# Reordering the low halves of h and splitting a weight's conversion between two engines, in a mixer kernel on one core

## The chip, the core and the metric

One core of a Trainium2 chip runs the whole program. The metric is the device time of one execution in microseconds (us). The kernel before has a median of 408.17 us over three runs (408.06 to 408.4).

The engines are named as the profile names them: PE (TensorE, matrix multiply), PEld (its weight loads), DVE (VectorE), ACT (ScalarE), POOL (GpSimd) and SP (SyncE, which here issues every DMA transfer; its queue is called SPq). Each engine works through its own list of instructions in order and waits at an instruction until the semaphores that it names have been raised.

## The reference, cut to what matters

```python
xn = _layernorm(x, axis=-1)                        # x: 1 x 2048 x 448
return x + A(xn, w_r, w_i) + B(xn, w1, w2, w3, w4)

# A: rfft2 of xn, times (w_r + 1j * w_i), irfft2
# B:
h  = gelu(_layernorm(x) @ w1)                      # 448 -> 448
# the four quarters of h are shifted by +1, -1, +2, -2 tokens -> hs
x1 = x + hs @ w2                                   # 448 -> 448
h2 = gelu(_layernorm(x1) @ w3) @ w4                # 448 -> 1792 -> 448
return x1 + h2
```

The change lies in the early part of B: the first normalisation, the product with w1, the shift, and the product with w2.

## The kernel before, in words

**Numbers in two halves.** Matrix products take fp16 operands. Every fp32 operand is split into a high half, its fp16 rounding, and a low half, the fp16 rounding of what is left. ACT usually writes the high half, and DVE or POOL subtracts it to get the low half.

**Blocks and groups.** The 2048 tokens stand in 16 blocks of 128 (token 16a + b is row a of one block), so that a shift by one or two tokens moves data from block to block, and only at the two ends from row to row. `GRP` puts the blocks in four groups of four: 14, 15, 0, 1, then 2 to 5, 6 to 9, and 10 to 13. The change speaks of the second group, blocks 2 to 5, and of the end of the first.

**One group's way.** `norm1(g)` takes statistics on DVE and ends in a scale and an offset for each block (`nma`, L328); the four blocks are then normalised by DVE and POOL (L336) and ACT (L333). Its second part, `refine`, computes the exact scale `gsc` on POOL (L343 to L352). `T1(g)` transposes the group on PE (L389), ACT takes the high half out of PSUM (L393) and DVE the low half (L394), into `xT`. Group 3 goes another way, `turn(3)`: ACT and DVE write halves of each block (L860 to L862), and a DMA transpose moves them to `xT` (L863).

**`w1_unit(g, i)`** multiplies block i of group g with w1 (11 matmuls, L420), then ACT computes gelu in place (L459) and the high half of h (L460). DVE computes the low half in two instructions (L462), k = 0 and k = 1. Both halves land shifted: `slots_of` spreads the four quarters of block c over the memory slots c-2, c-1 (k = 0) and c+1, c+2 (k = 1) of `x2mem`. A slot b is complete when its four neighbours have delivered. `DONE` names which slots are complete after which block, and for these the unit issues a DMA transpose on SP into `hT` (L470). So transpose 0 needs low halves from units (0,0) and (0,1), the first half of (0,3) and the first half of (1,0). It needs nothing from (0,2) itself.

**`w2_tile(b)`** multiplies the transposed slot b with w2: 11 matmuls (L478), the first six with the high and low halves of w2's first three pieces, then the low half of the fourth, then four with the pieces w2p[3] to w2p[6]. These four are copies of high halves, set together by two DMA moves inside `w2p` (L924, L925). DVE adds the product to x (L479), with a scale `cs` that POOL computes (L360 to L365). Tiles alternate between two PSUM banks, so tile 2 must wait until DVE has emptied the bank of tile 0.

**w2's halves.** POOL scales each piece (L276), ACT writes its high half (L277), POOL subtracts (L278). The four pieces are done in a row before the second group's units, and both moves are queued right behind them on SP.

**What sets the order.** Instructions are put on each engine's list by a scheduler that follows priorities and the order of the code; `behind(key)` keeps an instruction from being issued before another one has been. SP's list is in one order too, and a DMA transpose that waits holds back all transfers behind it. Behind the four transposes of the second group stand the loads of the last part of w3 (L223, two of 448 KB) and of w4 (L238, 1344 KB), and behind these the transposes of `turn(3)` and those of the next four slots.

Of the kernel before, what the change touches and what calls it, by code (L numbers as in the profile page):

```python
# [15 lines left out]
AF = mybir.ActivationFunctionType  # L16
ALU = mybir.AluOpType
# [108 lines left out]
def body(tc, nc, x, wf, w1, w2, w3, w4, c_g, c_n, c_small, out):  # L126
    V, A, P, T, SY = nc.vector, nc.scalar, nc.gpsimd, nc.tensor, nc.sync
# [28 lines left out]
    def bank(tag, name):  # L156
        return ps.tile([128, 512], F32, tag=tag, bufs=2, name=name)
# [19 lines left out]
    def stage(name, n, side, dtype=F32):  # L177
        t = pw.tile([128, 1808], F32, tag=f"stage{side}", bufs=1, name=name)
        return (t if dtype is F32 else t.bitcast(dtype))[:, :n]
# [25 lines left out]
    w2s = stage("w2s", F, 1).rearrange("p (t n) -> p t n", t=4)  # L205
# [49 lines left out]
    def powers(m, n, key, tag="acc", spare=0):  # L255

        t = pc.tile([128, 2], F32, name=f"pt{key}")
        after["r" + key] = (V.tensor_reduce(out=t[:, 0:1], in_=m[:, :n], axis=AX.X, op=ALU.add).ins,)
        pm = bank(tag, f"pm{key}") if isinstance(tag, str) else tag
        i = T.matmul(pm[:, 0:1], ones, t[:, 0:1], start=True, stop=True)  # L260
        after["p" + key] = (i.ins,)
        V.tensor_scalar(out=t[:, 1:2], in0=pm[:, 0:1], scalar1=2.0 ** -58, scalar2=None, op0=ALU.max)
        e = pc.tile([128, 3], I32, name=f"pe{key}")
        V.tensor_scalar(out=e[:, 0:1], in0=t.bitcast(I32)[:, 1:2], scalar1=1, scalar2=0x7F800000,
                        op0=ALU.logical_shift_right, op1=ALU.bitwise_and)
        V.tensor_scalar(out=e[:, 1:2], in0=e[:, 0:1], scalar1=-1, scalar2=185 - spare << 23, op0=ALU.mult, op1=ALU.add)
        i = V.tensor_scalar(out=e[:, 2:3], in0=e[:, 0:1], scalar1=1, scalar2=69 + spare << 23, op0=ALU.mult, op1=ALU.add)
        after["e" + key] = (i.ins,)
        return e.bitcast(F32)[:, 1:2], e.bitcast(F32)[:, 2:3]
# [4 lines left out]
    def split_w(hi, lo, src, s, low=None):  # L274
        if low is P:
            after["ps"] = (P.tensor_scalar(out=src, in0=src, scalar1=s, scalar2=0.0, op0=ALU.mult, op1=ALU.add).ins,)  # L276
            i = A.activation(out=hi, in_=src, func=AF.Copy)  # L277
            j = P.tensor_tensor(out=lo, in0=src, in1=hi, op=ALU.subtract)  # L278
            return i.ins, j.ins
        i = A.activation(out=hi, in_=src, func=AF.Copy, scale=s)  # L280
        j = V.scalar_tensor_tensor(out=lo, in0=src, scalar=s, in1=hi, op0=ALU.mult, op1=ALU.subtract)
        return i.ins, j.ins
# [89 lines left out]
    after = {}  # L372

    @contextlib.contextmanager
    def behind(*key):
        key = key if len(key) > 1 else key[0]
        with contextlib.ExitStack() as st:
            for i in after[key]:
                st.enter_context(tc.issue_after(i))
            yield  # L380
# [27 lines left out]
    w2p = pr.tile([128, 11, D], F16, name="w2p")  # L408
# [5 lines left out]
    def w1_in(g, units, ts, passes=range(3)):  # L414
        for p in passes:
            for t in ts:
                for i, pm in units:
                    wi, xi = ((0, 0), (0, 4), (4, 0))[p]
                    if t < 3 or p != 1:
                        m = T.matmul(pm[:, :D], xTs[g][:, xi + t, 128 * i:128 * i + 128], w1p[:, wi + t],  # L420
                                     start=t == 0 and p == 0, stop=t == 3 and p == 2)
        after["u"] = (m.ins,)

    def slot(b):
        return x2mem[:, 896 * b + 3584:896 * b + 4480].rearrange("p (i n) -> p i n", i=2)

    def slots_of(c, i):

        t = slot(c - 2)[:, i]
        return bass.AP(t.tensor, t.offset, [list(t.ap[0]), [3 * 896 + 224, 2], [896 + 112, 2], [1, 112]])  # L430
# [12 lines left out]
    def wrap_on():  # L443
        move(pairs[1], pairs[0], -1)

    def wrap_back():
        move(pairs[0], pairs[2], 1)
        for b, k in ((-2, slice(224, 448)), (-1, slice(336, 448))):
            P.tensor_copy(out=slot(b)[:, :, k], in_=slot(b - 2)[:, :, k])

    def w1_unit(g, i, pm=None):
        if pm is None:
            pm = bank(("tr" if g == 1 else "mm", "acc")[i // 2], f"pw1_{g}{i}")
            w1_in(g, [(i, pm)], range(4))
        c = CS[GRP[g][i]]
        pm = pm[:, :D]
        pv_ = pm.rearrange("p (i j n) -> p i j n", i=2, j=2)
        h = [slots_of((GRP[g][i] + 2) % NB - 2, k) for k in range(2)]
        A.activation(out=pm, in_=pm, func=AF.Gelu_apprx_tanh, scale=gsc[:, c:c + 1])  # L459
        u = A.activation(out=h[0], in_=pv_, func=AF.Copy, scale=h1)  # L460
        for k in range(2):
            v = V.scalar_tensor_tensor(out=h[1][:, k], in0=pv_[:, k], scalar=h1, in1=h[0][:, k],  # L462
                                       op0=ALU.mult, op1=ALU.subtract)
        after[g, i] = u.ins, v.ins
        for b in DONE.get(GRP[g][i], ()):
            if b == 14:
                wrap_back()
            if b // 4 not in hT:
                hT[b // 4] = pr.tile([128, 7, 512], F16, tag="h", bufs=2, name=f"h{b // 4}")
            d = SY.dma_start_transpose(out=hT[b // 4][:, :, 128 * (b % 4):128 * (b % 4) + 128],  # L470
                                       in_=slot(b if b < 14 else b - 16).rearrange("p i n -> p (i n)"))
            after["h", g, i] = (d.ins,)

    def w2_tile(b):
        pm = bank("sp", f"pw2_{b}")
        h = hT[b // 4][:, :, 128 * (b % 4):128 * (b % 4) + 128]
        for n, (k, w) in enumerate([(k, w) for k in range(3) for w in (k, k + 7)] + [(3, 10)] + [(k, k) for k in (3, 4, 5, 6)]):
            T.matmul(pm[:, :D], h[:, k], w2p[:, w], start=n == 0, stop=n == 10)  # L478
        V.scalar_tensor_tensor(out=xb(b), in0=xb(b), scalar=cs[:, CS[b]:CS[b] + 1], in1=pm[:, :D],  # L479
                               op0=ALU.mult, op1=ALU.add)  # L480
# [367 lines left out]
    def T1(g, ts=range(4)):  # L848
        if g not in xTs:
            xTs[g] = p1.tile([128, 7, 512], F16, tag="xT", bufs=2, name=f"xT{g}")  # L850
        transpose_split([xb(b) for b in GRP[g]], xTs[g], f"a{g}", ts,
                        tags=("mm", "mm", "tr", "tr") if g == 2 else ("tr", "tr", "acc", "acc"))
# [26 lines left out]
    first = [bank("mm" if k < 2 else "sp", f"pw1_0{k}") for k in range(4)]  # L879
# [9 lines left out]
    n = 2  # L889
# [11 lines left out]
    with behind("n", 1), behind("u"):  # L901
        s2, r2 = powers(m2, 1, "2", first[0][:, 448:512])
# [9 lines left out]
    for k in range(2):  # L912
        w1_unit(0, k, first[k])
    with behind("a1"):
        n1.append(norm1(2, [P, V, A, P], [("e2",), ("e2",), ("e2",), ("e2",)]))
    with behind("a1"), behind("n", 2):
        for k in range(2, 4):
            w1_unit(0, k, first[k])
    wrap_on()
    with behind("g", 1), behind("na", 2):  # L920
        for k in range(4):
            r = slice(0, 128 if k < 3 else 64)
            after["w2", k] = split_w(w2p[r, k], w2p[r, 7 + k], w2s[r, k], s2[r], P)
        SY.dma_start(w2p[64:128, 3:7], w2p[0:64, 0:4])  # L924
        SY.dma_start(w2p[0:64, 4:7], w2p[64:128, 0:3])  # L925
    with behind("w2", 3):
        P.memset(pairs[0][0:1], 0.0)
        P.memset(pairs[2], 0.0)
    for k in range(4):
        w1_unit(1, k)  # L930
    T1(2)
    with behind("h", 1, 3):
        load_w3([3])
# [174 lines left out]
```

## Time and profile before

| | |
|---|---|
| median of three runs | 408.17 us |
| the profiled execution | 408.05 us, of which the span of the profile is 406.3 us |
| PE busy | 399.9 us, 98% of the span |
| DVE, ACT, POOL busy | 82%, 63%, 25% of the span |
| granted clock of PE | 0.998 |

The span runs from the first to the last instruction of the profile; 1.75 us of the execution lie outside it. The page gives the busy time of each engine. A row of the timeline gives start, duration, engine, line, operation and tiles, the number of instructions merged into it, and in brackets how long the engine had been idle and what released it. A row of waits sums such idle time by who waited for whom. A matmul's end is modelled and overlaps with the next one, so that a row's duration is longer than the step from its start to the next start.

### The profile page before, as it was taken

Reading aid. Unit: us, or ns where it says so; the run is one execution under the profiler, and the core shown is the slowest. Engines: PE = TensorE matmul, PEld = TensorE weight load, DVE = VectorE, ACT = ScalarE, POOL = GpSimd, SP = SyncE. Lnnn points to the kernel's source line nnn. Section 1 sums busy time; section 2 is a strip of 40 time slices with the busy share of each in tenths; the row PEclk is TensorE's granted clock in tenths of the full one; section 3 lists DMA queues with packets and bytes.
Section 4 is the critical chain, followed back from the end, with each engine's and each line's share of the span. In section 5 each row is a group of like instructions: output and inputs, shape, how many; then the busy total and the mean of one; then the engine's idle time right before and its main releaser. Section 6 shows DMA issues by size and latency. Waiting matters only on the chain.

```text
span 406.3 us, 8732 instructions
## 1 busy us (share of the span) xinstructions
PE 399.9 (98%) x3391; PEld 297.2 (73%) x3391; DVE 333.6 (82%) x702; ACT 255.1 (63%) x433; POOL 100.4 (25%) x158
## 2 busy tenths in 40 slices
PE   8999999999999999999999999999999999999996
PEld 3555555865667877777878878777677779998995
DVE  5898799898947887988698888965999999965645
ACT  4788889874568857655698878853354544353431
POOL 6859910111146946500021111110000000000000
PEclk9999999999999999999999999999999999999999
DMA  8978975567489661637256556510011023100101
GB/s 280 389 272 160 249 152 138 122 121 163 95 225 266 234 191 46 219 95 185 72 144 164 162 142 161 139 27 2 24 69 70 24 90 92 47 2 2 45 2 45
DMA packets 54596, 52.07 MB, mean 128 GB/s; under 512 B 35678, under 2 KB 48542, under 8 KB 54556
## 3 DMA queue, kind: packets, MB, share of 16 engines
q1 hardware_dynamic: 54556, 51.53, 46.0%
q8 instruction: 26, 0.43, 0.4%
q14 instruction: 14, 0.11, 0.1%
HBM read 38.28 MB, written 3.67 MB: 103 GB/s over the span
## 4 chain that ended last, share of the span: by engine, by line
PE 87%; POOL 5%; DMA 2%; DVE 2%; ACT 2%; issue 1%; SPq 0%; POOLq 0%; ACTq 0%
PE pw L400 33%; PE acc L808 23%; PE pw L478 6%; PE side L778 4%; PE acc L778 3%; PE pu L667 3%; PE ps L567 3%; PE pe L688 2%; PE pp L622 2%; PE px L639 2%; PE py L709 2%; PE pw L420 2%; DMA w1s<-w 1%; POOL xt L336 1%; DMA h<-x2mem 1%
## 5 line engine op out<-in xcount | busy, mean ns | idle before, releaser
L400 PE MATMUL pw<-x2mem,w3p 128*128 128x256 f16 x1232 | 151.3, 273 | 0.0
L400 PEld LDWEIGHTS <-w3p 128*128 128x128 f16 x1232 | 118.9, 98 | 19.3
L808 PE MATMUL acc<-w4p,hf 128*128 128x448 f16 (+1 forms) x516 | 104.4, 348 | 0.0
L808 PEld LDWEIGHTS <-hf 128*128 128x128 f16 x516 | 50.1, 98 | 37.6
L726 ACT ACTIVATE pw<-pw,pe 128x512 f32<-128x512 f32 x42 | 27.4, 654 | 26.8 <-PE pw L400 26.6
L729 DVE SCALAR_TENSOR_TENSOR hf<-pw,h,hf 128x512 f16<-128x512 f32 x42 | 31.3, 746 | 12.9 <-ACT hf L728 12.7
L478 PE MATMUL pw<-w2p,h 128*128 128x448 f16 x176 | 35.8, 353 | 0.9 <-DMA h<-x2mem 0.9
L420 PE MATMUL pw<-w1p,xT 128*128 128x448 f16 x176 | 34.9, 352 | 0.1
L648 POOL TENSOR_TENSOR z<-te 128x450 f32<-128x450 f32 x16 | 15.7, 983 | 70.8 <-DVE te L646 65.9
L728 ACT ACTIVATE hf<-pw,h 128x512 f16<-128x512 f32 x42 | 28.9, 687 | 5.0 <-PE acc L808 4.0
L478 PEld LDWEIGHTS <-h 128*128 128x128 f16 x176 | 17.0, 98 | 17.0 <-DMA h<-x2mem 2.0
L744 ACT ACTIVATE hz<-g,h 128x896 f16<-128x896 f32 x14 | 14.6, 1044 | 23.1 <-DVE g L741 23.1
L420 PEld LDWEIGHTS <-xT 128*128 128x128 f16 x176 | 17.1, 99 | 16.1 <-DVE xT L394 0.4
L778 PEld LDWEIGHTS <-hz 128*128 128x128 f16 x294 | 28.3, 98 | 0.6
L629 ACT ACTIVATE pf<-pp 64x450 f16<-64x450 f32 x32 | 17.4, 544 | 12.5 <-DVE pf L630 9.7
L630 DVE TENSOR_TENSOR pf<-pp,pf 64x450 f16<-64x450 f32 x32 | 19.9, 622 | 5.1 <-ACT pf L629 4.7
L745 DVE SCALAR_TENSOR_TENSOR hz<-g,h,hz 128x896 f16<-128x896 f32 x14 | 16.1, 1148 | 6.8 <-ACT hz L744 6.8
L550 POOL TENSOR_TENSOR f<-xr 128x452 f32<-128x452 f32 x16 | 19.7, 1251 | 0.6
L558 DVE TENSOR_TENSOR xh<-f,xh 128x452 f16<-128x452 f32 x16 | 14.3, 916 | 5.7 <-ACT xh L557 5.7
L644 ACT ACTIVATE te<-px 64x450 f32<-64x450 f32 x32 | 17.3, 541 | 1.2 <-PE px L639 0.6
L738 ACT ACTIVATE g<-pw,pe 128x512 f32<-128x512 f32 x14 | 9.6, 683 | 11.3 <-PE pw L400 11.3
L547 POOL TENSOR_TENSOR xr<-xf 128x452 f32<-128x452 f32 x8 | 9.2, 1156 | 22.3 <-issue 16.4
(188 smaller groups left out, 705.7 us busy)
## 6 DMA issues: line engine op xcount, KB each, us to landing
wc<-wf SPq DMA_DIRECT2D x32, 225.0 KB, 3.7
wl<-wf SPq DMA_DIRECT2D x8, 450.0 KB, 4.3
xt<-x SPq DMA_DIRECT2D x8, 448.0 KB, 7.1
xf<-x SPq DMA_DIRECT2D x8, 448.0 KB, 4.6
loads<-x SPq DMA_DIRECT2D x7, 448.0 KB, 4.0
out<-xt SPq DMA_DIRECT2D x13, 224.0 KB, 1.9
w3raw<-w SPq DMA_DIRECT2D x3, 896.0 KB, 10.8
gn<-c_g SPq DMA_DIRECT2D x16, 128.0 KB, 3.0
```

The costliest lines, as they stand in the source:

```text
L400: T.matmul(ps_out, wp[:, wi + t, cols], xT[:, xi + t, tok], start=t == 0 and wi + xi == 0, stop=t == 3 and wi == 4)
L420: m = T.matmul(pm[:, :D], xTs[g][:, xi + t, 128 * i:128 * i + 128], w1p[:, wi + t], start=t == 0 and p == 0, stop=t == 3 and p == 2)
L478: T.matmul(pm[:, :D], h[:, k], w2p[:, w], start=n == 0, stop=n == 10)
L550: P.tensor_tensor(out=f[:, :, k:k + 2].rearrange("p b s d -> p s b d"), in0=u[:, :, 0], in1=u[:, :, 1], op=op)
L629: A.activation(out=hi, in_=src, func=AF.Copy)
L630: V.tensor_tensor(out=lo, in0=src, in1=hi, op=ALU.subtract)
L644: A.activation(out=e[64 * h:64 * h + 64], in_=px_[64 - 64 * h:128 - 64 * h, :2 * DF], func=AF.Copy)
L726: A.activation(out=pm, in_=pm, func=AF.Gelu_apprx_tanh, scale=r3)
L728: i = A.activation(out=h[:, 0], in_=pm, func=AF.Copy, scale=h3)
L729: j = V.scalar_tensor_tensor(out=h[:, 1], in0=pm, scalar=h3, in1=h[:, 0], op0=ALU.mult, op1=ALU.subtract)
L778: m = T.matmul(to, h[:, hi, 128 * blk:128 * blk + 128], b[wi], start=new and n == 0, stop=n == 2 and (last if blk in (2, 5, 3, 0) else end ...
L808: m = T.matmul(to, h[:, hi, o:o + 128], w4p[0][:, wi, f, r], start=first and f % 2 == 0 and n == 0, stop=end and f % 2 == 1 and n == 2, sk ...
```

## The change

The low half of h can be written one instruction at a time: `w1_unit` gets an argument `ks` and returns a function `low(k)`. The second group's code then orders these by which transpose needs them first. The conversion of w2 is taken apart: pieces 0 and 1 get their high half on ACT as before, piece 0 ahead of the second group's gelus, and pieces 2 and 3 get it on DVE (a cast from fp32 to fp16). The low halves of w2 stay on POOL. The two moves of w2 are issued behind the first transpose by an explicit rule.

```diff
-    def w1_unit(g, i, pm=None):
+    def w1_unit(g, i, pm=None, ks=range(2)):
...
-        for k in range(2):
+        def low(k):
             v = V.scalar_tensor_tensor(out=h[1][:, k], in0=pv_[:, k], scalar=h1, in1=h[0][:, k],
                                        op0=ALU.mult, op1=ALU.subtract)
-        after[g, i] = u.ins, v.ins
+            after[g, i] = u.ins, v.ins
+        for k in ks:
+            low(k)
...
+        return low
...
-        for k in range(2, 4):
-            w1_unit(0, k, first[k])
+        lows = {(0, k): w1_unit(0, k, first[k], ()) for k in range(2, 4)}
+        lows[0, 3](0)
     wrap_on()
-    with behind("g", 1), behind("na", 2):
+    r = [slice(0, 128)] * 3 + [slice(0, 64)]
+    with behind("g", 1):
         for k in range(4):
-            r = slice(0, 128 if k < 3 else 64)
-            after["w2", k] = split_w(w2p[r, k], w2p[r, 7 + k], w2s[r, k], s2[r], P)
+            P.tensor_scalar(out=w2s[r[k], k], in0=w2s[r[k], k], scalar1=s2[r[k]], scalar2=0.0, op0=ALU.mult, op1=ALU.add)
+    def w2_hi(k, e):
+        if e is V:
+            return V.tensor_copy(out=w2p[r[k], k], in_=w2s[r[k], k]).ins
+        return A.activation(out=w2p[r[k], k], in_=w2s[r[k], k], func=AF.Copy).ins
+    def w2_lo(k):
+        with behind("np", 2):
+            after["w2", k] = (P.tensor_tensor(out=w2p[r[k], 7 + k], in0=w2s[r[k], k], in1=w2p[r[k], k], op=ALU.subtract).ins,)
+    w2_hi(0, A)
+    w2_lo(0)
+    lows[1, 0] = w1_unit(1, 0, None, (0,))
+    with behind("n", 2):
+        lows[0, 2](1)
+    lows[1, 1] = w1_unit(1, 1, None, (0,))
+    with behind("n", 2):
+        for unit, k in (((0, 3), 1), ((1, 0), 1), ((0, 2), 0)):
+            lows[unit](k)
+    with behind("na", 2):
+        w2_hi(1, A)
+    w2_lo(1)
+    with behind("n", 2):
+        w2_hi(2, V)
+    w2_lo(2)
+    with behind("n", 2):
+        w2_hi(3, V)
+    w2_lo(3)
+    with behind("h", 1, 0):
         SY.dma_start(w2p[64:128, 3:7], w2p[0:64, 0:4])
         SY.dma_start(w2p[0:64, 4:7], w2p[64:128, 0:3])
...
-    for k in range(4):
-        w1_unit(1, k)
+    lows[1, 2] = w1_unit(1, 2, None, (0,))
+    lows[1, 1](1)
+    lows[1, 3] = w1_unit(1, 3, None, (0,))
+    for k in range(2, 4):
+        lows[1, k](1)
```

**On DVE**, from the statistics of the third group to the first low half of its transposes (`xT<-pta`), the list before was as follows. `pw_10` is the PSUM tile of unit (1,0), and so on; a low half of 224 columns reads as 128x2x112.

```order
L326 TENSOR_SCALAR vy<-va 128x2x4
L462 SCALAR_TENSOR_TENSOR x2mem<-pw_10_440,h_252,x2mem 128x2x112 x2
L327 TENSOR_SCALAR vy<-vy 128x2x4
L328 SCALAR_TENSOR_TENSOR nma<-mva,vy 128x4
L336 TENSOR_SCALAR xt_79<-xt_79,vy,nma 128x448
L462 SCALAR_TENSOR_TENSOR x2mem<-pw_02_211,h_252,x2mem 128x2x112 x2
L462 SCALAR_TENSOR_TENSOR x2mem<-pw_03_212,h_252,x2mem 128x2x112 x2
L462 SCALAR_TENSOR_TENSOR x2mem<-pw_11_458,h_252,x2mem 128x2x112 x2
L394 TENSOR_TENSOR xT_509<-pta_510,xT_509 128x512
```

And the same place in the changed program:

```order
L464 SCALAR_TENSOR_TENSOR x2mem<-pw_10_427,h_252,x2mem 128x2x112
L327 TENSOR_SCALAR vy<-vy 128x2x4
L328 SCALAR_TENSOR_TENSOR nma<-mva,vy 128x4
L336 TENSOR_SCALAR xt_79<-xt_79,vy,nma 128x448
L464 SCALAR_TENSOR_TENSOR x2mem<-pw_03_212,h_252,x2mem 128x2x112
...
L464 SCALAR_TENSOR_TENSOR x2mem<-pw_02_211,h_252,x2mem 128x2x112
L933 CAST w2p<-w2s 128x448
L933 CAST w2p<-w2s 64x448
L464 SCALAR_TENSOR_TENSOR x2mem<-pw_11_445,h_252,x2mem 128x2x112 x2
L464 SCALAR_TENSOR_TENSOR x2mem<-pw_12_474,h_252,x2mem 128x2x112 x2
L394 TENSOR_TENSOR xT_509<-pta_510,xT_509 128x512
```

One low half has moved from before `nma` to behind the normalisation. The half of (0,3) that transpose 0 needs is the first behind the normalisation, where it was the third. Five single halves come ahead of the two casts, and unit (1,1) follows the casts.

**On SP**, the list from the first transpose of h to the second of the next four slots (`h_598`) was, before:

```order
L470 DMA_TRANSPOSE h_456<-x2mem 128x7x128
L924 DMA w2p<-w2p 64x1792
L925 DMA w2p<-w2p 64x1344
L470 DMA_TRANSPOSE h_456<-x2mem 128x7x128 x3
L223 DMA w3raw<-w 64x1792 x2
L238 DMA w4half<-w 128x6x448
L863 DMA_TRANSPOSE xT_720<-x_721 128x7x128
L470 DMA_TRANSPOSE h_598<-x2mem 128x7x128
L863 DMA_TRANSPOSE xT_720<-x_721 128x7x128 x2
```

In the changed program it reads:

```order
L475 DMA_TRANSPOSE h_442<-x2mem 128x7x128
L960 DMA w2p<-w2p 64x1344
L959 DMA w2p<-w2p 64x1792
L475 DMA_TRANSPOSE h_442<-x2mem 128x7x128 x3
L223 DMA w3raw<-w 64x1792 x2
L238 DMA w4half<-w 128x6x448
L869 DMA_TRANSPOSE xT_720<-x_721 128x7x128 x2
L475 DMA_TRANSPOSE h_598<-x2mem 128x7x128
L869 DMA_TRANSPOSE xT_720<-x_721 128x7x128 x2
```

The moves have changed places with each other. Further on, two transposes of `turn(3)` now stand ahead of the transpose of slot 4, where one stood.

**On PE**, the end of the third group's transposes and the start of tile 0 (`pw_0`) read before:

```order
L389 MATMUL pta_524<-ident,xt_80 128x128 x2
L389 MATMUL pta_531<-ident,xt_79 64x128 x2
L389 MATMUL pta_531<-ident,xt_80 64x128 x2
L478 LDWEIGHTS h_456
L478 MATMUL pw_0_668<-w2p,h_456 128x448
```

And in the changed program:

```order
L389 MATMUL pta_524<-ident,xt_80 128x128 x2
L484 LDWEIGHTS h_442
L484 MATMUL pw_0_668<-w2p,h_442 128x448
...
L389 MATMUL pta_531<-ident,xt_79 64x128 x2
L389 MATMUL pta_531<-ident,xt_80 64x128 x2
```

Three matmuls of tile 0 now stand ahead of the last quarter of the transposes, and 20 matmuls instead of 17 lie between the transposes and tile 1. Tile 4 is at the same place in PE's list as before.

## The prediction, made before the changed kernel was run

> **What bounds the kernel now.** I read the page's first section, then who waited for whom on PE, then PE's timeline around the change, then the chain of work that ended last, and then SP's and DVE's timelines there. First the page and PE's waits (total, times, longest, in us):
>
> ```profile
> PE 399.9 (98%) x3391; PEld 297.2 (73%) x3391; DVE 333.6 (82%) x702; ACT 255.1 (63%) x433; POOL 100.4 (25%) x158
> PE pw L478 <- DMA h<-x2mem: 0.9, 3, 0.4
> 54.00:406.00 352.00, 349.01 (x3122) 270.08 (x3120) 290.53 (x567) 214.15 (x360) 60.66 (x67) 1.00 0.40 107
> ```
>
> PE is busy 98% of the span. After 54 us it is busy 349.01 of 352 us (the last row: window, length, busy time of PE, PEld, DVE, ACT, POOL, clock, DMA share, GB/s), and nothing in the list of waits stops it there but the drain at the end. The change removes no matmul. So it can only win PE's waits in its own stretch, which are the three of w2's tiles (L478) for a transposed h. PE's timeline shows where the three are:
>
> ```profile
> 31.45 1.91 PE L389 MATMUL pta<-ident,xt 128*128 128x128 f32 x16
> 33.72 1.31 PE L478 MATMUL pw<-w2p,h 128*128 128x448 f16 x6 [0.36 <-DMA h<-x2mem]
> 36.00 1.11 PE L478 MATMUL pw<-w2p,h 128*128 128x448 f16 x5
> 37.39 2.26 PE L478 MATMUL pw<-w2p,h 128*128 128x448 f16 x11 [0.28 <-DMA h<-x2mem]
> 46.67 4.33 PE L478 MATMUL pw<-w2p,h 128*128 128x448 f16 x22
> 51.21 2.25 PE L478 MATMUL pw<-w2p,h 128*128 128x448 f16 x11 [0.22 <-DMA h<-x2mem]
> ```
>
> Tile 0 waits at 33.72, tile 1 at 37.39, tile 4 at 51.21. The idle time shown is a little short, because a matmul's modelled end overhangs: eleven take 2.26 us, but 37.39 plus eleven steps is 39.48, where the next row begins, so 0.19 us a step, and the end hangs over by 0.16 us. The three waits are really 0.52, 0.44 and 0.38 us, together 1.34 us. **That is all that can be won, 0.33% of 408.05 us.** A difference of 0.2%, 0.8 us, is about what a measurement of this kernel can tell from no change.
>
> The last of the three waits counts most, since it lies behind the others: the chain that ended last runs through it (start, length).
>
> ```profile
> 45.51 1.06 DVE xt L479 x2
> 46.57 4.60 DMA h<-x2mem
> 51.21 2.25 PE pw L478 x11
> ```
>
> Tile 4 starts when the transpose of slot 4, issued at 46.57, has landed. If that landing stays where it is, whatever PE wins at tiles 0 and 1 is spent waiting at tile 4.
>
> **The change, part by part.** The DVE rows first, then SP's with their landing times (the rows that end in a size and a number are issues: KB each, us to landing):
>
> ```profile
> 28.28 0.44 DVE L462 SCALAR_TENSOR_TENSOR x2mem<-pw,h,x2mem 128x224 f16<-128x224 f32 x1
> 28.64 0.16 DVE L327 TENSOR_SCALAR vy<-vy 128x8 int32<-128x8 int32 x1
> 29.03 0.51 DVE L336 TENSOR_SCALAR xt<-xt,vy,nma 128x448 f32<-128x448 f32 x1
> 29.46 2.24 DVE L462 SCALAR_TENSOR_TENSOR x2mem<-pw,h,x2mem 128x224 f16<-128x224 f32 x6
> 33.40 0.69 DVE L394 TENSOR_TENSOR xT<-pta,xT 128x512 f16<-128x512 f32 x1 [1.71 <-ACT xT L393]
> 29.88 1.97 ACT L277 ACTIVATE w2p<-w2s 128x448 f16<-128x448 f32 x4
> 30.68 1.34 SPq L470 DMA_TRANSPOSE h<-x2mem  x1
> DMA to landing us min/median/max: 3.0/3.0/3.0
> 32.13 0.53 SPq L924 DMA_DIRECT2D w2p<-w2p  x1
> 33.39 4.36 SPq L470 DMA_TRANSPOSE h<-x2mem  x3
> 37.80 1.22 SPq L223 DMA_DIRECT2D w3raw<-w  x2
> ```
>
> *Transpose 0.* The low half at 28.28 moves behind the normalisation, so `nma` and L336 come one step, 0.36 us, earlier: L336 at 28.67. Six low halves take 2.24 us, 0.36 us a step. The half of (0,3) that transpose 0 needs was third behind L336 and is now first: it ended at 29.46 + 2 x 0.36 + 0.44 = 30.62, which is when SP issued (30.68), and will end at 29.10 + 0.44 = 29.54. Issue at 29.6, landing 3.0 us later at 32.6. PE does three quarters of the transposes by 32.76 (12 of 16 steps of 0.11 from 31.45) and then starts tile 0: no wait. **Minus 0.52 us at tile 0**, covered by 0.15 us.
>
> *The moves of w2.* They were issued at 32.13, once ACT had written all four high halves (29.88 + 1.97). Now the gate is DVE's casts: five low halves from 29.10 end their steps at 30.9, then two casts. No row shows this cast. The nearest are L336 (one fp32 input of 448 columns, 0.51 us) above, and a statistics pass of the same size at 0.61 us and an fp16 copy of 1024 columns at 0.42 us below, so a cast lies between 0.4 and 0.6 us; I take 0.5, by L336. The first cast ends near 31.4, the second near 31.9. The first move now needs only three high halves, so it goes at 31.5 and the second right behind, 0.6 us earlier than before.
>
> ```profile
> L306 DVE BATCH_NORM_STATS2 sta<-xt 128x6 f32<-128x448 f32 x4 | 2.2, 614 | 0.0
> L680 DVE COPY U<-y 113x1024 f16<-113x1024 f16 x8 | 2.8, 421 | 0.0
> ```
>
> The casts cost DVE 1.0 us, hidden by the 1.71 us in which it sat idle before 33.40, waiting for ACT. ACT is relieved of two of the four activations of L277, 1.0 us, and moves a third to a place where it waited, so the quarters of `xT` come no later. If that cover were gone, the matmuls of units (2,0) to (2,3) would wait, still inside the slack at tile 4 below.
>
> *Transposes 1 to 3 and the loads.* They follow the moves on SP. The half of (1,1) that transpose 1 needs ends near 32.3, so SP goes on without a pause: 32.6 instead of 33.39, and with the same 4.36 us for three issues the loads of w3 and w4 start near 37.0 instead of 37.80, **0.8 us earlier**. Tile 1 starts after 20 matmuls, four transposes among them, near 37.0 (32.76 + 20 x 0.19 + 4 x 0.11); transpose 1 landed 3.9 us after its issue, which would now be 36.5. **Minus 0.44 us at tile 1.** PE is then 0.96 us ahead.
>
> *Tile 2.* It needs the bank of tile 0, which DVE empties at 45.51 + 0.67 = 46.2, held by POOL's scale `cs`. POOL starts 0.36 us earlier with the same work, but the scales now follow the next normalisation and one more small operation ahead of them: 46.1. PE arrives at 46.67 - 0.96 = 45.7 and waits 0.4 us. So 0.56 us are left, and PE arrives at tile 4 at 46.1 + 22 x 0.19 = 50.3.
>
> *Tile 4.* SP's rows, the landing times of the two transposes that start at 44.65 and 46.57 and of the next, those of w4's load, and what the DMA engines did meanwhile:
>
> ```profile
> 39.07 0.59 SPq L238 DMA_DIRECT2D w4half<-w  x1
> 44.65 1.82 SPq L863 DMA_TRANSPOSE xT<-x  x1
> 46.57 1.83 SPq L470 DMA_TRANSPOSE h<-x2mem  x1
> 48.51 2.85 SPq L863 DMA_TRANSPOSE xT<-x  x2
> w4half<-w SPq DMA_DIRECT2D x1, 1344.0 KB, 10.6
> xT<-x SPq DMA_TRANSPOSE x1, 5.8
> h<-x2mem SPq DMA_TRANSPOSE x1, 4.6
> xT<-x SPq DMA_TRANSPOSE x1, 3.5
> 46.00:47.00 1.00, 1.00 (x7) 0.50 (x6) 1.00 (x4) 1.00 (x3) 0.69 (x4) 1.00 1.05 373
> 48.00:49.00 1.00, 1.00 (x7) 0.54 (x6) 1.00 (x4) 1.00 (x3) 1.00 (x5) 1.00 0.42 32
> 49.50:50.50 1.00, 1.00 (x7) 0.54 (x6) 1.00 (x6) 1.00 (x3) 0.90 (x4) 1.00 1.28 286
> ```
>
> The last load lands at 39.07 + 10.6 = 49.6. The three transposes land at 50.4, 51.2 and 52.0: one every 0.8 us behind the load, however long before they were issued. So slot 4 is not held by its data but by the queue: the load's end plus two transposes. In the change it stands behind two transposes instead of one. **The load ends 0.8 us earlier, and one more transpose of 0.8 us stands ahead:** slot 4 lands at 49.6 - 0.8 + 3 x 0.8 = 51.2, give or take 0.2 us. I take 51.05, since the SP issue may gain up to 1.0 us (three issues in 4.36 us held one pause for DVE). PE waits from 50.3 to 51.1.
>
> *The sum.* -0.52 - 0.44 (tiles 0 and 1) + 0.4 (tile 2) + about 0.45 more at tile 4 (0.8 instead of 0.38) gives -0.1 us. Against the profiled execution that is 408.05 - 0.1 = 407.95; the median of before is 0.12 us above it, so I say **408.0 us**, within 0.2%. Its own range, with the queue 0.5 us either way: 407.5 to 408.6.
>
> **Rivals.**
>
> *The queue does not take it back (faster).* Between 48 and 49 us the DMA engines moved 32 GB/s after 373 GB/s: the tail of the load on few engines, with the transposes stuck. If that tail is not there, slot 4 lands by 50.3 and tile 2's bank is the last wait: 51.21 - 50.3 gives -0.9 us, 407.1. For it: 1.5 us of nearly idle DMA. Against it: the same load stands in the same place of the same queue.
>
> *The casts wait for POOL (slower).* DVE and POOL slow each other in this trace when both normalise:
>
> ```profile
> 18.22 1.26 DVE L336 TENSOR_SCALAR xt<-xt,vy,nma 128x448 f32<-128x448 f32 x2
> 18.30 0.94 POOL L336 TENSOR_SCALAR xt<-xt,vy,nma 128x448 f32<-128x448 f32 x1
> 41.81 1.42 POOL L336 TENSOR_SCALAR xt<-xt,vy,nma 128x448 f32<-128x448 f32 x2
> 30.96 1.04 POOL L278 TENSOR_TENSOR w2p<-w2s,w2p 128x448 f16<-128x448 f32 x1
> ```
>
> POOL's 0.71 us became 0.94, and DVE's pair took 1.26 us where two steps of 0.43 and a tail would be 0.94. The casts fall on POOL's subtractions of 1.04 us each. A cast that waits out half of one costs 0.5 us more, the pair 1.0; SP's 0.8 us are then lost and 0.2 more, and with the extra transpose slot 4 lands at 52.2: +1.0 us, 409.1. It decides from 0.8 us of waiting on. If each cast waited out a whole subtraction it would be +2. The Trainium skill ("SBUF — State Buffer", section "Who interferes with whom") says that a cast on VectorE in a 2-port mode and a GpSimd instruction hold a shared port pair alone, whoever starts first. The pair at 18.22 agrees with that, and by that rule this rival would be the rule here; but the five halves ahead read PSUM, and POOL's small operations between its subtractions leave gaps, so I hold it less likely than not.
>
> *The moves are not earlier (no gain at all).* If SP's order is bound elsewhere, the load ends where it did and only the extra transpose is left: +0.8 us, 408.9.
>
> **How the numbers follow.** The queue as worked out: 0.55, nearly all within 0.2%. The missing tail: 0.18, faster. Casts waiting: 0.18, mostly slower by over 0.2%. Moves not earlier: 0.09, half of it slower. So faster 0.20, same 0.58, slower 0.22. The range goes from the missing tail (407.1) to the casts' half waits (409.1), widened by 0.1 us for the spread of runs.
>
> **What would show it.** Right: no wait of PE at tiles 0 and 1; the issue of transpose 0 near 29.6, of the first move near 31.5, of w4's load near 38.2; a wait of about 0.4 us before tile 2 that names DVE, and a longer one than before at tile 4 that names the DMA of h; slot 4's transpose landing 0.8 us behind the second of `turn(3)`. Wrong: casts far above 0.6 us or POOL's subtractions above 1.04 (second rival); a landing of slot 4 before 50.5 (first); a new wait of PE behind 54 us, since the scheduler also reordered later stretches, which I count at nothing because the list of waits has none of PE there.

## The result and the profile after

| | before | after |
|---|---|---|
| median of 12 runs each | 408.12 us (407.9 to 408.81) | 409.39 us (408.32 to 410.03) |
| ratio, 95% interval | | 1.0026 (1.0018 to 1.0033) |
| profiled execution | 408.05 us, span 406.3 | 409.47 us, span 407.7 |

The change costs 1.27 us between the medians. I had forecast 408.0 us and a range that ended at 409.2. PE's waits and its timeline around the change, of the kernel after (w2's tiles are L484 now), come first:

```profile
PE pw L484 <- DMA h<-x2mem: 0.7, 1, 0.7
PE pw L484 <- DVE xt L485: 0.5, 1, 0.5
```

```profile
31.44 1.47 PE L389 MATMUL pta<-ident,xt 128*128 128x128 f32 x12
32.75 0.73 PE L484 MATMUL pw<-w2p,h 128*128 128x448 f16 x3
...
36.02 3.07 PE L484 MATMUL pw<-w2p,h 128*128 128x448 f16 x14
...
46.58 4.32 PE L484 MATMUL pw<-w2p,h 128*128 128x448 f16 x22 [0.49 <-DVE xt L485]
51.61 2.25 PE L484 MATMUL pw<-w2p,h 128*128 128x448 f16 x11 [0.71 <-DMA h<-x2mem]
```

The wait at tile 0 is gone: it starts at 32.75, 0.97 us earlier than before. The wait at tile 1 is gone from the list, but 0.25 us of it are left in steps. Two others stand in their place. Tile 2 waits for the bank that DVE empties and starts at 46.58, only 0.08 us earlier than before. Tile 4 waits for the DMA of h and starts at 51.61 instead of 51.21. From there on PE runs 0.39 to 0.40 us late to its last matmul.

That is 0.4 of 1.4 us. The rest is behind PE's last matmul. DVE's last rows and the DMA of the last stretch (402 to 406.9 us), of after:

```profile
402.28 1.60 DVE L821 SCALAR_TENSOR_TENSOR xt<-acc,p,xt 128x448 f32<-128x448 f32 x3 [1.25 <-PE acc L814]
```

```profile
q1 hardware_dynamic: 432, 0.46, 27.4%
q14 instruction: 1, 0.01, 0.7%
...
out<-xt SPq DMA_DIRECT2D x2, 112.0 KB, 2.3
```

The same two views of before:

```profile
401.90 1.60 DVE L815 SCALAR_TENSOR_TENSOR xt<-acc,p,xt 128x448 f32<-128x448 f32 x3 [1.25 <-PE acc L808]
```

```profile
q1 hardware_dynamic: 432, 0.46, 27.2%
issues: line engine op xcount, KB each, median us to landing
...
out<-xt SPq DMA_DIRECT2D x2, 112.0 KB, 1.8
```

From the end of DVE's last row to the end of the span it is 2.84 us before (403.50 to 406.34) and 3.80 us after (403.89 to 407.69). After has a packet there that before hasn't: one load of instructions (q14), 8192 bytes, from 405.28 to 405.81 us. The last output transfer lands between 405.51 and 405.66 on fifteen of its sixteen DMA engines and at 406.67 on the sixteenth. The packets in the trace show how: there are 48 packets of 4 bytes, one for each engine and output transfer, which close its share. Of the last transfer's sixteen, fifteen have ended by 405.30, and one goes at 405.80, just as the load of instructions ends. Before, the same kind of load came at 407.00, behind the end of the span. So the profiled executions differ by 0.39 us on PE, 0.96 behind it and 0.07 outside the span: 1.42.

### The profile page after: what moved, and what is told of

Its sections match the earlier page's. It is cut to its first block, busy times and chain, and to the rows that moved or that the text cites. A ratio compares the mean times of both kernels' runs of the same rounds, so it can differ in the third digit from the quotient of the medians.

```text
span 407.7 us, 8731 instructions
## 1 busy us (share of the span) xinstructions
PE 400.2 (98%) x3391; PEld 297.6 (73%) x3391; DVE 334.7 (82%) x704; ACT 254.1 (62%) x431; POOL 101.0 (25%) x158
## 4 chain that ended last, share of the span: by engine, by line
PE 89%; POOL 5%; DVE 2%; ACT 1%; issue 1%; DMA 1%; POOLq 0%
PE pw L400 33%; PE acc L814 23%; PE pw L484 6%; PE side L784 4%; PE acc L784 3%; PE pu L673 3%; PE ps L573 3%; PE pe L694 2%; PE pp L628 2%; PE px L645 2%; PE py L715 2%; PE wps L844 2%; PE pw L420 2%; POOL xt L336 1%; POOL w2p L938 1%
## 5 line engine op out<-in xcount | busy, mean ns | idle before, releaser
L484 PE MATMUL pw<-w2p,h 128*128 128x448 f16 x176 | 36.4, 352 | 1.3 <-DMA h<-x2mem 0.7
L484 PEld LDWEIGHTS <-h 128*128 128x128 f16 x176 | 17.1, 98 | 16.7 <-DMA h<-x2mem 1.7
L563 ACT ACTIVATE xh<-f 128x452 f16<-128x452 f32 x16 | 8.7, 573 | 9.5 <-POOL f L556 7.8
```

## The experiments

Two theories were to be tested. **A:** the tail is the load of instructions, whose place follows VectorE's count of instructions (832 records of VectorE in the trace before, its semaphore instructions included, and 834 after). **B:** tile 4's 0.4 us is slot 4's place in SP's queue. The rivals: the tail belongs to the changed order or is just the price of more VectorE work; tile 4 waits for its data or for the tile before. "Tail" is always the time from the end of DVE's last row to the end of the span.

**Two VectorE instructions more in the kernel before.**

```diff
     V.memset(m2, 0.0)
+    pad = pc.tile([128, 2], F32, name="pad")
+    for i in range(2):
+        V.memset(pad[:, i:i + 1], 0.0)
```

> The kernel before with two more one-column memsets on VectorE at the very start, where it waits for the first load; every other instruction stands as before. Theory (instruction load at the end): the changed kernel's last output transfer is held up by an 8 KB instruction load at 405.28 us, which before came at 407.00, behind the end; it is triggered by VectorE's count of instructions, which the change raised by two. Then this kernel shows an 8 KB load between 404 and 406 us, PE as before (last matmul group at 398.3), and a time 0.8 to 1.2 us above before in most runs. Rival (the last transfer is late by chance, or because of what the change does earlier): time as before, within 0.2 us, load behind the end.

408.33 us, ratio 1.0011 (1.0003 to 1.002). The last stretch, 402 to 406.9 us:

```profile
q1 hardware_dynamic: 432, 0.46, 27.3%
q14 instruction: 1, 0.01, 0.6%
...
out<-xt SPq DMA_DIRECT2D x2, 112.0 KB, 1.9
```

The load moved as A says, from 407.00 to 405.12 us, for two memsets at the start of the program. Its price was not constant, and the 0.8 to 1.2 us that I expected in most runs came in a few: the profiled tail was 3.04 us, and of the eleven runs seven were between 407.9 and 408.52 us and four between 409.07 and 409.33. The profiled execution is one of the seven, and its packets show why it was cheap: the load began at 405.125 us, and the last of the output's 4-byte packets had ended at 405.112. In the changed kernel the load began at 405.278, ahead of the last of them. So in these two executions a few hundredths of a microsecond separate the cheap case from the dear one. That the load stood ahead in the other four is likely, but they were not profiled.

**Two VectorE instructions fewer in the changed kernel.**

```diff
-    V.memset(warm, 0.0)
-    A.activation(out=warm, in_=warm, func=AF.Gelu_apprx_tanh)
...
+    A.activation(out=warm, in_=ones[:, 0:1], func=AF.Gelu_apprx_tanh)
...
-    V.memset(m1, 0.0)
-    V.memset(m2, 0.0)
+    V.memset(m12, 0.0)
```

> The changed kernel with two VectorE instructions fewer at the start (two memsets merged into one, and the first activation fed from another constant). Theory: VectorE's count is that of before, the 8 KB load comes behind the end again, the last transfer lands about 1.8 us after its issue, and the time falls by 1.0 us to 0.4 us above before (408.5). Rival (late by chance or by the change's other parts): 409.4 as the changed kernel.

408.72 us, 1.0016 (1.0005 to 1.0027). The load went back behind the end (407.48), the tail to 2.83 us, and PE still reached tile 4 0.34 us late. In the profiled executions the two costs are separate. The medians alone would not show it: the interval overlaps that of the changed kernel, and four of the twelve runs lay between 409.03 and 409.94 us, which the profiled execution does not explain.

**Fourteen VectorE instructions more in the changed kernel.** If a load just ahead of the end is harmful, one that comes much earlier must be harmless, though the kernel then does more.

```diff
             after["f", G, fp] = i.ins, j.ins
+            if G in (3, 4):
+                with behind("f", G, fp):
+                    V.memset(pad[:, 7 * G - 21 + fp:7 * G - 20 + fp], 0.0)
```

> The changed kernel with fourteen one-column memsets more on VectorE, placed where VectorE idles in the middle of the program; the order of every other engine is the changed kernel's. Theory (the last load of VectorE's instructions falls among the output's last transfer and holds it): it comes fourteen instructions earlier, several us ahead of the last output, so the time from VectorE's last instruction to the end of the span falls from 3.80 us to the 2.8 to 2.9 of the kernel before, PE's last matmul stays where the changed kernel has it (+0.4), and the time is about 408.6, though the kernel does more. Rival (the later end is just the price of more VectorE instructions, or of the stretch at tile 4 alone): the tail stays at 3.8 and the time at 409.4 or above.

408.54 us, 1.0006 (0.9998 to 1.0015), 0.85 us under the changed kernel's median. The last stretch, 402 to 406.9 us, where no row of q14 is left:

```profile
q1 hardware_dynamic: 432, 0.46, 27.5%
issues: line engine op xcount, KB each, median us to landing
...
out<-xt SPq DMA_DIRECT2D x2, 112.0 KB, 1.8
```

The load came at 393.29 us and the tail fell to 2.77 us. More instructions made the kernel faster (the interval ends below that of the changed kernel), and the order on all other engines was the changed kernel's. Not all of the 0.85 us is the tail: PE's last matmul also came 0.17 us earlier than in the changed kernel, counted from the second group's transposes. A holds.

**Slot 4's transpose ahead of the second of `turn(3)`.** Only SP's order changes, by one place.

```diff
-            d = SY.dma_start_transpose(out=xTs[g][:, :, 128 * i:128 * i + 128], in_=h)
+            with behind("h", 2, 0) if i else contextlib.nullcontext():
+                d = SY.dma_start_transpose(out=xTs[g][:, :, 128 * i:128 * i + 128], in_=h)
```

> The changed kernel with one edit in SyncE's list: the transpose of slot 4 stands again ahead of the second transpose of turn(3), as before the change. Theory (queue: slot 4 lands 0.8 us per transpose behind the load of w4): it lands near 50.8 instead of 51.57, PE starts tile 4 near 50.85 instead of 51.61 with a wait of about 0.1, and the time falls by 0.75 us against the changed kernel, to 0.35 below before plus the 1.0 us at the end (408.7). Rival (slot 4 is held by its own data or by SyncE's issue): landing near 51.5, time as the changed kernel, 409.4.

408.68 us, 1.0013 (1.0004 to 1.0022). PE's timeline:

```profile
46.51 6.53 PE L484 MATMUL pw<-w2p,h 128*128 128x448 f16 x33 [0.54 <-DVE xt L485]
```

Tiles 2, 3 and 4 run as one row of 33: the wait at tile 4 is gone. The load landed at 49.00 us, the transpose ahead at 49.77, slot 4 at 50.55, the same steps of 0.77 to 0.78 us, with one step fewer than in the changed kernel. Counted from the start of the second group's transposes, tile 4 starts at 31.67 us (before 31.92, after 32.33). B holds. The tail stayed at 3.79 us, as A has it for 834: the load began at 404.45, and the last 4-byte packet of the output went when it ended, at 404.91.

**Both edits.**

> Both edits together: slot 4's transpose ahead of the second one of turn(3), and two VectorE instructions fewer. If both theories hold and their terms add, 409.4 - 1.0 - 0.75 = 407.65 to 407.8, 0.3 to 0.5 us below before (0.1%). If only the order on SyncE counts, 408.7; if only the instruction load counts, 408.5.

408.12 us, ratio 1.0 (0.9991 to 1.0009), tail 2.87 us. With both costs taken out the kernel is level with before. I had expected 0.3 to 0.5 us less: counted from the second group's transposes PE's last matmul came 0.29 us earlier than before, but the median shows nothing of it. That the time is 0.1 us from the forecast for the changed kernel is chance, since that forecast was for another order on SP.

**The first part of the change alone:** the low halves, with all of w2's high halves on ACT as before. Against the changed kernel, where the calls of `w2_hi` and `w2_lo` go as well:

```diff
-        for k in range(4):
-            P.tensor_scalar(out=w2s[r[k], k], in0=w2s[r[k], k], scalar1=s2[r[k]], scalar2=0.0, op0=ALU.mult, op1=ALU.add)
+        with behind("na", 2):
+            for k in range(4):
+                after["w2", k] = split_w(w2p[r[k], k], w2p[r[k], 7 + k], w2s[r[k], k], s2[r[k]], P)
```

> The first part of the change alone: the low halves one by one in the order of the transposes, and w2's moves held behind the first transpose; w2's high halves all on ScalarE as before, so VectorE has as many instructions as before. The scheduler then puts slot 4's transpose ahead of all four of turn(3). Theory: no wait of PE at tile 0 (0.5 us won); slot 4 lands one transpose, 0.8 us, behind the load, near 50.4, so tile 4 waits for nothing or under 0.2 us; the tail stays at 2.8 us since the count of VectorE's instructions is that of before; time 407.6 to 408.0. Rival (the casts moved to VectorE are what brings w2 and the loads forward, without them the loads come later): load lands at 49.6 or later, and the time is 408.1 or above.

407.75 us, 0.9989 (0.998 to 0.9998): the better half of the change. PE's timeline:

```profile
33.09 0.73 PE L484 MATMUL pw<-w2p,h 128*128 128x448 f16 x3
...
35.48 1.31 PE L484 MATMUL pw<-w2p,h 128*128 128x448 f16 x6 [0.62 <-DMA h<-x2mem]
...
46.84 6.41 PE L484 MATMUL pw<-w2p,h 128*128 128x448 f16 x33
```

The load landed at 49.67 us, no earlier than before (49.62), as the rival had it. But slot 4 landed at 50.45, one step behind it, since here the scheduler put it ahead of all four transposes of `turn(3)`. So tile 4 follows without a wait. The tail was 2.76 us. One thing was not foreseen: in the middle of tile 0 PE now waits 0.62 us, to 35.48. The matmuls there are the first six of tile 1, which PE's list has ahead of tile 0's last five, and they wait for transpose 1, which landed at 35.44. POOL's last subtraction ended at 35.45, but the matmul that waits for it comes only at 37.76.

**The second part alone:** the casts on VectorE, with the low halves in pairs as before. Against the changed kernel:

```diff
-        lows = {(0, k): w1_unit(0, k, first[k], ()) for k in range(2, 4)}
-        lows[0, 3](0)
+        for k in range(2, 4):
+            w1_unit(0, k, first[k])
...
-    lows[1, 0] = w1_unit(1, 0, None, (0,))
...
+    w1_unit(1, 0)
```

> The second part of the change alone: two of w2's high halves on VectorE and the moves behind the first transpose, with the low halves in pairs in the order of before. Slot 4's transpose stands behind one of turn(3), as before. Theory: tile 0 waits its 0.5 us as before (its half is third behind the normalisation again), the load of w4 is issued within 0.2 us of before, so tile 4 starts within 0.2 us of before; but VectorE has two instructions more, so the last load of its instructions falls on the last output and the tail is 3.8 us; time 408.7 to 409.1. Rival (the later tail belongs to the changed order and not to the count): tail 2.8 us and time 408.1.

409.23 us, 1.0028 (1.0019 to 1.0038). The time is near what I expected, and the reason is not. The tail was 2.79 us: the order of this version needs fewer semaphore instructions on VectorE, 831 records in all, and the load came at 408.28, behind the end. Tile 4 started 0.16 us earlier than before, counted from the second group's transposes. PE's last matmul was 0.81 us late all the same. Its timeline shows two waits behind tile 4:

```profile
55.82 0.36 PE L484 MATMUL pw<-w2p,h 128*128 128x448 f16 x1 [0.20 <-DVE pt L262]
...
80.61 1.69 PE L484 MATMUL pw<-w2p,h 128*128 128x448 f16 x8 [0.45 <-DMA h<-x2mem]
```

In steps they are 0.36 and 0.61 us, which with the 0.16 won make the 0.81. The scheduler reordered later stretches here. So this run says nothing on A, except that the number of arithmetic instructions (704, as in the changed kernel) is not the count that matters.

**Further: the scale earlier, then slot 4 first.** Tile 2's wait was to go by putting POOL's `cs` ahead of two normalisations, on top of both edits above.

```diff
-        P.tensor_scalar(out=c, in0=c, scalar1=s12[:, 0:1], scalar2=None, op0=ALU.mult)
+        i = P.tensor_scalar(out=c, in0=c, scalar1=s12[:, 0:1], scalar2=None, op0=ALU.mult)
+        after["cs", g] = (i.ins,)
...
+                with behind("cs", 0) if g == 3 and k > 1 else contextlib.nullcontext():
```

> The changed kernel with slot 4's transpose ahead of the second of turn(3), two VectorE instructions fewer, and GpSimd's scale cs ahead of the third and fourth normalisation of the last group. Theory: tile 2 no longer waits for the bank that VectorE empties (0.5 us shown, 0.65 in steps), tile 4 is then bound by slot 4's landing near 50.6, so 0.2 to 0.5 us are won over the kernel with the two edits alone, whose median was 408.12: 407.7 to 407.9. Rival (PE's later start of tile 2 was cover for something behind it, as the normalisations that now come later): a new wait of PE behind tile 4 gives it back, 408.1 or more.

408.02 us, 0.9995 (0.9986 to 1.0004), against 407.7 to 407.9 expected. Tile 2 started 0.7 us earlier than with the two edits, and tile 4 then waited 0.51 us for slot 4. The next version takes `if i` out of the edit on SP's order, so that slot 4 stands ahead of all four:

> As the version with both edits and the earlier scale (408.02 us), but slot 4's transpose stands ahead of all four of turn(3). Theory: slot 4 now lands one transpose behind the load of w4, near 50.2 instead of 50.95, and PE, whose tile 2 starts near 46.1, reaches tile 4 near 50.3 and does not wait for it, so another 0.5 us is won: 407.4 to 407.7, and no wait of PE at a w2 tile. Rival (the transposes of turn(3) that now come later hold the units (3,0) to (3,3), which stood behind tile 4): a new wait of PE between 51 and 60 us, and 408.0 or more.

407.96 us, 0.9994 (0.9986 to 1.0003). PE's timeline:

```profile
46.17 4.33 PE L485 MATMUL pw<-w2p,h 128*128 128x448 f16 x22
50.68 2.24 PE L485 MATMUL pw<-w2p,h 128*128 128x448 f16 x11 [0.18 <-DVE xt L486]
```

Slot 4 landed at 49.99 us and the wait for it was gone, and PE's last matmul came 0.68 us earlier than before, counted as above. Yet the median says 0.1 us. In all twelve of its runs 2.12 to 2.21 us lay outside the span, where the median before is 1.72. VectorE had 829 records, and its last load ran from 407.43 to 407.98 us, 2.2 us behind the end of the span; before it ended 1.2 us behind. So the last version has the fourteen memsets too:

> The version with slot 4's transpose first and the scale earlier, with fourteen one-column memsets more on VectorE in the middle of the program, where it idles; the order of every other engine is unchanged. That version's span was 405.81 us, 0.53 shorter than that of the kernel before, but its time was shorter by only 0.1: 2.13 us lie outside its span instead of 1.71. Theory (its last load of VectorE's instructions, from 407.47 to 408.02, is still under way when the rest has ended, and the execution ends with it): with the load moved into the middle of the last stretch, near 393 us, the span stays at 405.8 and the time falls to 407.5, which would be the fastest of all. Rival (what lies outside the span has another cause): 407.9 again.

407.63 us, 0.9986 (0.9977 to 0.9995). The span is the same 405.8 us, and 1.80 us lie outside it (median) instead of 2.15. The median time is 0.33 us lower; the two intervals overlap, so the share outside the span shows the gain more clearly than the time does.

**The low halves alone with the fourteen memsets.**

> The low halves alone, with the same fourteen memsets. Its load ended at 407.81 us, 1.79 behind the end of the span, and 1.80 us lie outside its span. Theory (the load sets the end only where it ends later than about 1.75 us behind the span): nothing or 0.1 us to win, 407.6 to 407.8. Rival (every load behind the end costs its own 0.3 to 0.5 us): 407.3 to 407.4.

407.56 us, 0.9987 (0.9979 to 0.9996), with 1.80 us outside the span (1.79 without the memsets). That is 0.19 us less than without them, just below the 407.6 to 407.8 expected. It lies in the span (405.8 instead of 406.0), not outside it, and within the two intervals, so no gain of the memsets is shown here. This version and the one before it, with slot 4 first and the fourteen memsets, beat both kernels, by 0.13 to 0.14% against before, and are alike within their intervals.

## Why the prediction was wrong, point by point

*Tile 0.* Right. Transpose 0 was issued at 29.54 (forecast 29.6), tile 0 started at 32.75 (32.76).

*The casts and the rival of POOL's port: the step that failed first.* "The first cast ends near 31.4, the second near 31.9." The two casts and the two subtractions of POOL beside them, one row for each, of after:

```profile
30.37 1.03 POOL L938 TENSOR_TENSOR w2p<-w2s,w2p 128x448 f16<-128x448 f32 x1
30.83 0.82 DVE L933 CAST w2p<-w2s 128x448 f16<-128x448 f32 x1
31.57 0.38 DVE L933 CAST w2p<-w2s 64x448 f16<-64x448 f32 x1
31.68 1.18 POOL L938 TENSOR_TENSOR w2p<-w2s,w2p 128x448 f16<-128x448 f32 x1
```

And of the second part alone (`w1_w2_part_alone`):

```profile
30.84 1.03 POOL L938 TENSOR_TENSOR w2p<-w2s,w2p 128x448 f16<-128x448 f32 x1
30.93 1.18 DVE L933 CAST w2p<-w2s 128x448 f16<-128x448 f32 x1
```

As a group the casts have a mean of 0.60 us, close to the 0.5 forecast. But the group mixes two: the second cast took 0.38 us, the first, of as many columns on 128 partitions instead of 64, took 0.82. The first began inside a subtraction of POOL and ended 0.25 us behind its end (31.40 and 31.65). In the second part alone it began 0.37 us earlier within the subtraction, took 0.36 us longer, and again ended 0.25 us behind it. The distance is 0.25 us in all nine kernels that have the casts. So the first cast waited for POOL: 0.44 us, if a cast alone takes 0.38. POOL in turn lost 0.15 us on the subtraction that began during the second cast (1.18 instead of 1.03). The rival of the casts came true for one cast of two. That is less than the 0.8 us of waiting from which it was to decide, and that its 409.1 is near the measured time is luck, since most of the loss lies at the end. The Trainium skill ("SBUF — State Buffer", section "Who interferes with whom") says that a cast in a 2-port mode and a GpSimd instruction exclude each other, whoever starts first; this trace agrees, with 0.82 against 0.38 us. In which mode the cast ran no run shows.

*Transposes 1 to 3 and the loads: what followed from it, and a second size.* The forecast was that "the loads of w3 and w4 start near 37.0 instead of 37.80", 0.8 us earlier. SP's rows of after:

```profile
31.72 0.53 SPq L960 DMA_DIRECT2D w2p<-w2p  x1
32.34 0.55 SPq L959 DMA_DIRECT2D w2p<-w2p  x1
32.98 4.36 SPq L475 DMA_TRANSPOSE h<-x2mem  x3
37.39 1.22 SPq L223 DMA_DIRECT2D w3raw<-w  x2
38.66 0.59 SPq L238 DMA_DIRECT2D w4half<-w  x1
...
48.09 1.53 SPq L475 DMA_TRANSPOSE h<-x2mem  x1
```

The first move came at 31.72 instead of 31.5, right behind the end of the first cast (31.65): 0.22 us are the cast's wait. From the first move to the three transposes it is 1.26 us (31.72 to 32.98), and before it was 1.26 us too (32.13 to 33.39). I had taken 1.1, and part of it for a pause that the change removes. It is the two moves themselves, with 0.62 and 0.64 us to the next issue: the other 0.16 us. So everything behind moved by the same 0.41 us and not 0.8. An estimate from these rows: without the wait of 0.44 us the first move would have gone near 31.3 and the loads 0.85 us earlier than before, about the gain that I forecast. No run took the wait away.

*Tiles 1 and 2.* The same step at work: transpose 1 was issued at 32.98 instead of 32.6, took 4.19 us instead of 3.9, and landed at 37.17 instead of the forecast 36.5. So tile 1 still waited 0.25 us in steps (before 0.44) and began at 37.22. Tile 2 started at 46.58 instead of 46.1. DVE's row of after for the bank:

```profile
45.85 1.27 DVE L485 SCALAR_TENSOR_TENSOR xt<-xt,cs,pw 128x448 f32<-128x448 f32 x2 [1.09 <-POOL cs L365]
```

DVE emptied the bank from 45.85 on (before 45.51), because POOL ended `cs` at 45.81. I had taken POOL to be 0.36 us earlier there and to lose 0.26 of it. But its `gsc` (L352) came only 0.14 us earlier than before, and the four normalisations that stand ahead of `cs` in both kernels took about 0.3 us longer. It cost nothing more in the end, since 46.58 and 22 steps of 0.19 make 50.76, still ahead of slot 4.

*Tile 4.* Right in mechanism, off in size. Slot 4's transpose stands behind the load and two others, as forecast. The chain of after:

```profile
48.09 3.48 DMA h<-x2mem
51.57 0.05 issue
51.61 2.25 PE pw L484 x11
```

The load landed at 49.22 instead of the forecast 48.8, the transposes at 49.99, 50.77 and 51.57, in steps of 0.77 to 0.80. With the load where it was, the same sum gives 51.6. That is +0.4 on the time in place of -0.1. The rival of the missing tail did not come (a landing before 50.5), and the rival of the moves that come no earlier came by half: they came 0.41 us earlier, not 0 and not 0.6.

*The end: the step that failed most.* The prediction spoke of "later stretches, which I count at nothing because the list of waits has none of PE there." PE indeed had no new wait there. But the end of the program isn't PE's: 2.84 us pass behind DVE's last instruction before the span ends, and there two instructions more were not free, because they moved a load of instructions onto the last output. That cost 0.96 us in the profiled execution, and 0.67 and 0.85 us in the medians of the runs that took it away. Without it the time would have stayed within the range, as it did with the fourteen memsets (408.54).

## What to carry to other kernels

A wait that is removed from an in-order queue is worth only what the next entry of the queue gives back: follow the queue to the transfer that the end of the stretch waits for, and price an issue by the step to the next one, not by its row's length. When a change adds or removes instructions on an engine, look where its last load of instructions falls: next to the last output it cost about 1 us here, and in four of eleven runs two one-column memsets were enough for that. When two engines work side by side, read each of their rows, not the mean of a group that holds two shapes: a mean of 0.60 us hid a wait of 0.44. And test such a suspicion with harmless instructions, a few more and many more, before believing in either the new order or the new work.

## What the runs showed of the hardware that was not expected

- Loads of VectorE's instructions (q14, taken for VectorE's because they move with its count) come 8192 bytes at a time and use the same DMA engines as data. With 830 to 832 records of VectorE the last load came at 406.9 to 408.3 us, with 834 at 404.45 to 405.28, with 843 to 848 at 392.7 to 398.7. With 834 one engine's share of the output landed up to 1.0 us behind the other fifteen: where the load began ahead of that engine's last packet of 4 bytes, this packet went only when the load had ended. The Trainium skill ("Runtime: NRT & Kernel Launch", section "Instruction fetch mechanics") says that the sequencer fetches its own program through a DMA queue in blocks of 16 KiB, and that the cost of crossing a block is "mostly hidden". These runs agree on the queue; VectorE's blocks here had 8 KiB (16 KiB on another queue, q8), and at the end of the program the cost was not hidden.
- A load may also come too late: with 829 records it ended 2.0 to 2.2 us behind the span, and 2.15 us (median of 23 runs) lay outside the span instead of 1.7. Where the limit lies is open: with 831 records the load ended 1.58 us behind the span and 1.89 us lay outside, with 830 it ended 1.79 behind and 1.79 lay outside.
- DMA transposes that were issued early land one every 0.8 us (the first two 0.75 to 0.82) behind a load of 1344 KB, whatever their own issue time.
- A cast on VectorE that began inside a subtraction on GpSimd ended 0.25 us behind the subtraction's end, whether it began 0.09 or 0.46 us into it: it took 1.18 and 0.82 us, against 0.38 for the cast behind it.

What stays open: of the runs with two memsets added to the kernel before, the four near 409.2 us were not profiled, so that the load stood ahead of the last 4-byte packet in them is argued from three profiled executions. No run gave the first cast a start outside POOL's subtraction, so what its wait cost in time is an estimate. That w1's part alone makes the later waits through the scheduler's reordering, and not through the casts themselves, was read from its trace and not tested by itself.
